# Four squares instead of three in a run of attention matmuls, from chunk 4 on, in a kernel of windowed attention and a feed-forward block

## The chip, the core and the metric

The kernel runs on one core of one Trainium2 chip. The metric is the device time of one execution in microseconds (us); the time of the kernel before is 961.14 us, the median of three runs. The profile is of one further execution.

## What is computed

Attention with 8 batches, 8 heads, 576 positions and head size 64 looks back over a window of 64 positions. Its output, 4608 rows of 512 numbers, goes through a feed-forward block with 2048 hidden units. All is in 32-bit floats.

```python
scores = scale * np.matmul(q, k.transpose(0, 1, 3, 2))
mask = (rel >= 0) & (rel < window)
attn = np.exp(scores - max); attn = attn / (np.sum(attn, axis=-1, keepdims=True) + 1e-09)
x = np.matmul(attn, v)  # 4608 x 512
h = x @ w_in            # 512 x 2048
out = (h * np.tanh(np.log1p(np.exp(h)))) @ w_out   # 2048 x 512
```

## The kernel before

**Chunks and steps.** The 4608 rows are cut into 12 chunks of 384 (CH). The feed-forward block takes a chunk in 16 steps (NF). One step is `ffn_in` (L208), 12 matmuls of 128x384 into one bank `h_ps` (three per quarter of the input, since inputs and weights are split into a high and a low part, `xh`, `xl` and `wi_h`, `wi_l`), and `ffn_out` (L246), nine matmuls of 128x512 into three accumulators `acc`. `ffn_out` runs two steps behind `ffn_in` (LAG). Between the two, the hidden values of a step pass through a chain: DVE takes `t` out of `h_ps` (L223), ACT applies four functions (L224, L229, L230, L231), DVE multiplies by `h_ps` again (L233), POOL splits the product into `gh` and `gl` (L237, L238). There are two banks of `h_ps`, so the chain of step n must have passed L233 before `ffn_in` of step n+2 can write that bank.

**Attention.** A chunk has 4 head pairs (NPAIR), and a pair has 3 squares: 128 queries (two blocks of 64) by 128 keys, for two heads. `att_scores` (L130) issues 12 matmuls for a pair into two banks `s_ps`; each is 64x64 by 128, in one corner of the array. Then come, for each of the 6 squares and heads, a masked minimum on DVE (L150, into `pr` and `mx`) and an exponential with its row sum on ACT (L153, into `pr` and `sm`), and for all six together the normalisation on DVE (L161 to L163). From chunk 3 on `att_transpose` (L166) transposes 32x32 pieces on DVE (L173, `pr` to `tr`) and puts the pieces in place with 12 small DMAs on SP's queue (L178, `tr` to `pT`). `att_values` (L190) issues 12 matmuls of 128x64 by 64 into a bank `o_ps`, the first of which waits for all 12 DMAs, and then ACT and DVE split the result into `xh` and `xl` (L205, L206).

A float32 matmul stands as two records in the trace, so the 12 matmuls of a pair appear as x24.

**What sets the order.** PE's order is the order of the program: the loop over steps at L405 calls `ffn_in` of step n, then the attention events that are due (`run(2 * n)`, L412), then `ffn_out` of step n-2, then `run(2 * n + 1)`. Half a step is a slot. `Att.plan` (L324) gives each pair of a chunk three events: scores at its slot, transpose 0.6 of a spacing later, values one spacing later, just ahead of the scores of the next pair. The attention of chunk c begins 6 slots ahead of the feed-forward block of chunk c-1 and must end 6 slots ahead of that of chunk c; from chunk 4 on that is 32 slots for 4 pairs (L401). Values of one pair and scores of the next so stand together, behind an `ffn_in`; I call this place a visit. The other engines' orders are laid out by a scheduler behind these events; the code of the feed-forward chain and of L205 and L206 has higher priority.

**Loads and buffers.** After the scores of pair p come the loads of `q_t` and `k_t` of pair p+2, after its values that of `v_t` (L297), each with two buffers. `pr` and `tr` share a ring of two (`tag="pr"`). There are two `pT`, zeroed once (L86). The output tiles `o` of `ffn_store` (L254) have a ring of three (`tag="st"`), used before that by the loading of weights. Attention has three PSUM banks (`tag="at"`).

Of the kernel before, what the change touches and what calls it, by code (L numbers as in the profile page):

```python
# [10 lines left out]
F32 = mybir.dt.float32  # L11
F32R = mybir.dt.float32r
# [3 lines left out]
ALU = mybir.AluOpType  # L16

P = 128
BLK = 64
TINY = float(np.array(0x38000000, np.uint32).view(np.float32))  # L20
BIG = float(np.array(0x47EFFFFF, np.uint32).view(np.float32))
SYNC = mybir.DependencyInfo(mybir.DependencyClass.Sync, mybir.DependencyReason.DATA)
SOON = 400
# [4 lines left out]
def tile_window_attn_mish_ffn(  # L28
# [10 lines left out]
    nc = tc.nc  # L39
    NPAIR, _, NT = qT.shape  # L40
    NF, _, NC_, _ = w_in.shape
    DO = w_out.shape[2]
    CH = 384
# [3 lines left out]
    NM = NB // 2  # L47
    HM = 2 * NM
    LAG = 2

    const = ctx.enter_context(tc.tile_pool(name="const", bufs=1))
    xp = ctx.enter_context(tc.tile_pool(name="xp", bufs=1))
    ap_ = ctx.enter_context(tc.tile_pool(name="ap_", bufs=2))
    mp = ctx.enter_context(tc.tile_pool(name="mp", bufs=2))
    ps_acc = ctx.enter_context(tc.tile_pool(name="ps_acc", bufs=1, space=bass.MemoryType.PSUM))
    ps_h = ctx.enter_context(tc.tile_pool(name="ps_h", bufs=2, space=bass.MemoryType.PSUM))
    ps_at = ctx.enter_context(tc.tile_pool(name="ps_at", bufs=3, space=bass.MemoryType.PSUM))
# [16 lines left out]
    for j in range(2):  # L74
        m = const.tile([P, P], F32, name=f"mask{j}")
# [7 lines left out]
    wo_l = const.tile([P, NF, DO], F32R, name="wo_l")  # L83


    pTs = [const.tile([P, P // 32, HM, 32], F32, name=f"pT{i}") for i in range(2)]  # L86
    for t in pTs:
        nc.gpsimd.memset(t, 0.0)
    pTs = itertools.cycle(pTs)


    order = []
    ordered = []

    def pe(*args, **kw):
        order.append(nc.tensor.matmul(*args, **kw).ins)  # L96

    def in_order():
        return tc.issue_after(order[-1]) if ordered else nullcontext()
# [6 lines left out]
    def bank(c, p, name):  # L106
        if c == 2 or (c == 0 and p % 2 == 0):
            return ps_acc.tile([P, CH], F32, name=name, tag=next(sums))
        return ps_at.tile([P, CH], F32, name=name, tag="at")
# [17 lines left out]
                                       ap=[[P, P], [BLK * P, NB], [1, P]]))  # L127
        return v_t

    def att_scores(c, p, tiles):  # L130
        q_t, k_t = tiles
        s_ps = [bank(c, p, "s_ps").rearrange("p (m k) -> p m k", k=P) for _ in range(2)]
        pr = ap_.tile([P, HM, P], F32, name="pr", bufs=2)
        mx = ap_.tile([P, HM], F32, name="mx", bufs=3)
        sm = ap_.tile([P, HM], F32, name="sm", bufs=3)
        for m in range(NM):
            for par, h in ((0, 0), (1, 1), (1, 0), (0, 1)):
                n = 2 * m + par
                rows = slice(h * BLK, (h + 1) * BLK)
                pe(s_ps[h][par * BLK:(par + 1) * BLK, m, :],  # L140
                   q_t[rows, n * BLK:(n + 1) * BLK], k_t[rows, n * BLK:n * BLK + P],
                                 start=True, stop=True)
        for h in range(2):
            js = slice(h * NM, (h + 1) * NM)
            for m in range(NM):
                first = [(c * NB + 2 * m + par) % blocks_per_seq == 0 for par in range(2)]
                mk = firsts[first.index(True)] if any(first) else mask
                j = h * NM + m

                nc.vector.tensor_tensor_reduce(  # L150
                    out=pr[:, j, :], in0=s_ps[h][:, m, :], in1=mk,
                    op0=ALU.add, op1=ALU.min, scale=-0.125, scalar=3.0e38, accum_out=mx[:, j:j + 1])
                nc.scalar.activation(pr[:, j, :], pr[:, j, :], AF.Exp, bias=mx[:, j:j + 1], scale=-1.0,  # L153
                                     accum_out=sm[:, j:j + 1])
            if c == 0:

                nc.vector.tensor_scalar(sm[:, js], sm[:, js], 1e-9, None, ALU.add)
                nc.vector.reciprocal(sm[:, js], sm[:, js])
                nc.vector.tensor_tensor(pr[:, js, :], pr[:, js, :], sm[:, js].unsqueeze(2).to_broadcast([P, NM, P]), ALU.mult)
        if c > 0:  # L160
            nc.vector.tensor_scalar(sm, sm, 1e-9, None, ALU.add)  # L161
            nc.vector.reciprocal(sm, sm)
            nc.vector.tensor_tensor(pr, pr, sm.unsqueeze(2).to_broadcast([P, HM, P]), ALU.mult)  # L163
        return pr

    def att_transpose(c, p, pr):  # L166
        pT = next(pTs)
        if c > 2:


            moved = []
            tr = ap_.tile([P, P // 32, HM, 32], F32, name="tr", tag="pr", bufs=2)
            nc.vector.transpose(tr.rearrange("p k j i -> p j k i"),  # L173
                                pr.rearrange("p j (k i) -> p j k i", i=32))
            for r in range(0, P, 32):
                for k in range(0, P, 32):
                    if 0 <= k - r % BLK <= BLK:
                        moved.append(nc.sync.dma_start(pT[k:k + 32, r // 32, :, :], tr[r:r + 32, k // 32, :, :]))  # L178
            return pT, moved
        for h in range(2):  # L180
            t_ps = (bank(c, p, "t_ps") if c else ps_h.tile([P, CH], F32, name="t_ps", tag="h_ps")
                    ).rearrange("p (m k) -> p m k", k=P)
            for m in range(NM):
                order.append(nc.tensor.transpose(t_ps[:, m, :], pr[:, h * NM + m, :], ident).ins)
            (nc.scalar.copy if h == 0 else nc.vector.tensor_copy)(
                pT[:, :, h * NM:(h + 1) * NM, :].rearrange("p r m i -> p m r i"),
                t_ps.rearrange("p m (r i) -> p m r i", i=32))
        return pT, []
# [101 lines left out]
    class Att:  # L290
# [17 lines left out]
        def scores(self, p):  # L308
            with in_order(), self.early():
                self.pr[p] = att_scores(self.c, p, self.qk[p])  # L310
            self.load(p + 2, "qk")

        def transpose(self, p):
            with in_order(), self.early():
                self.pT[p] = att_transpose(self.c, p, self.pr.pop(p))

        def values(self, p):
# [3 lines left out]
                att_values(self.c, p, self.v[p], self.pT.pop(p), self.x)  # L321
            self.load(p + 2, "v")

        def plan(self, begin, step, turn=0.6, lag=1):  # L324

            for p in range(NPAIR):
                at = begin + p * step
                events.extend([(at, 2, self.scores, p), (at + turn * step, 1, self.transpose, p),
                               (at + lag * step, 0, self.values, p)])

    events = []

    def run(slot):
        while events and events[0][0] <= slot:
            _, _, fn, p = events.pop(0)
            fn(p)
# [34 lines left out]
    starts = {c: 2 * len(steps) + 2 * NF * (c - 2) for c in range(2, NCHUNK)}  # L371
    steps += [(c, f) for c in range(2, NCHUNK) for f in range(NF)]

    atts = [Att(c) for c in range(NCHUNK)]
# [19 lines left out]
    ahead = 6  # L394
    begin = starts[2] + ahead - 1
    for c in range(3, NCHUNK):
        if c == 3:

            atts[c].plan(begin, (starts[c] - ahead - begin) / (NPAIR + 0.5), lag=1.5)
        else:  # L400
            atts[c].plan(begin, (starts[c] - ahead - begin) / NPAIR)  # L401
        begin = starts[c] - ahead
    events.sort(key=lambda e: e[:2])
    ordered.append(True)
# [52 lines left out]
```

## Time and profile before

| | |
|---|---|
| timed runs | 960.49, 961.14, 962.45 us |
| profiled execution, first to last instruction | 963.3 us |
| TensorE (PE) busy | 919.2 us, 95% |
| VectorE (DVE) busy | 491.9 us, 51% |
| ScalarE (ACT) busy | 622.1 us, 65% |
| GpSimd (POOL) busy | 330.3 us, 34% |
| granted PE clock, mean | 0.983 |

The span is the profiled execution's own time; no other time of it is known, and it stands 2.2 us above the median of the timed runs. In rows of the timeline the columns are the start in us from the span's start, the duration in us, the engine, the line and operation, what is written and read, the shape and the count (several instructions merged), and in brackets the idle time of the engine ahead of it with what ended it. PEld is the weight load on PE. SPq is the issuing of DMAs on SP's queue.

### The profile page before, as it was taken

Reading aid. Unit: us, or ns where it says so; the run is one execution under the profiler, and the core shown is the slowest. Engines: PE = TensorE matmul, PEld = TensorE weight load, DVE = VectorE, ACT = ScalarE, POOL = GpSimd, SP = SyncE. Lnnn points to the kernel's source line nnn. Section 1 sums busy time; section 2 is a strip of 40 time slices with the busy share of each in tenths; the row PEclk is TensorE's granted clock in tenths of the full one; section 3 lists DMA queues with packets and bytes.
Section 4 is the critical chain, followed back from the end, with each engine's and each line's share of the span. In section 5 each row is a group of like instructions: output and inputs, shape, how many; then the busy total and the mean of one; then the engine's idle time right before and its main releaser. Section 6 shows DMA issues by size and latency. Waiting matters only on the chain.

```text
span 963.3 us, 18036 instructions
## 1 busy us (share of the span) xinstructions
PE 919.2 (95%) x6408; PEld 812.7 (84%) x6408; DVE 491.9 (51%) x1352; ACT 622.1 (65%) x1525; POOL 330.3 (34%) x419
## 2 busy tenths in 40 slices
PE   4687899999999999999999999999999999999997
PEld 2576788978889988988898988898889888898996
DVE  6797788264545445444545444544544454442322
ACT  5575777676666666657666666665766756665664
POOL 2143555332333333333233233333333323333333
PEclk9789999999999999999999999999999999999999
DMA  7554332032233213213222222311312312300000
GB/s 246 158 195 137 131 104 73 22 117 84 78 89 101 56 51 107 61 54 90 76 55 79 85 56 67 97 53 54 115 51 55 114 50 56 96 16 13 33 1 34
DMA packets 82650, 77.35 MB, mean 80 GB/s; under 512 B 10368, under 2 KB 73856, under 8 KB 82560
## 3 DMA queue, kind: packets, MB, share of 16 engines
q1 hardware_dynamic: 82560, 76.19, 26.1%
q8 instruction: 51, 0.84, 0.4%
q14 instruction: 39, 0.32, 0.1%
HBM read 56.10 MB, written 9.44 MB: 68 GB/s over the span
## 4 chain that ended last, share of the span: by engine, by line
PE 79%; DVE 10%; ACT 4%; DMA 2%; issue 2%; SPq 2%; ACTq 0%; POOL 0%; DVEq 0%; POOLq 0%
PE h_ps L96 37%; PE acc L96 36%; PE o_ps L96 3%; PE s_ps L96 3%; DVE wa L277 2%; DMA st<-w_out 2%; SPq L178 1%; DVE wa L278 1%; DVE t L233 1%; ACT pr L153 1%; DVE wa L276 1%; DVE pr L150 1%; DVE pr L163 1%; ACT t L229 1%; DVE wa L274 1%
## 5 line engine op out<-in xcount | busy, mean ns | idle before, releaser
L96 PE MATMUL h_ps<-xh,wi_h 128*128 128x384 f32 x768 | 262.9, 342 | 5.6 <-DVE t L233 5.1
L224 ACT ACTIVATE t<-t 128x384 f32<-128x384 f32 x192 | 100.6, 524 | 259.3 <-DVE t L223 259.2
L237 POOL TENSOR_SCALAR gh<-t 128x384 fp32r<-128x384 f32 x176 | 90.8, 516 | 513.8 <-DVE t L233 491.5
L96 PE MATMUL h_ps<-xh,wi_l 128*128 128x384 f32 x768 | 259.8, 338 | 0.0
L96 PE MATMUL h_ps<-xl,wi_h 128*128 128x384 f32 x768 | 259.5, 338 | 0.0
L96 PE MATMUL acc<-wo_h,gh 128*128 128x512 f32 x576 | 230.3, 400 | 0.5 <-POOL gh L237 0.5
L96 PE MATMUL acc<-wo_l,gh 128*128 128x512 f32 x576 | 226.2, 393 | 0.0
L233 DVE SCALAR_TENSOR_TENSOR t<-t,h_ps 128x384 f32<-128x384 f32 x176 | 97.2, 552 | 237.9 <-ACT t L231 233.3
L238 POOL TENSOR_TENSOR gl<-t,gh 128x384 fp32r<-128x384 f32 x192 | 201.5, 1050 | 35.7 <-ACT gh L235 21.0
L96 PE MATMUL acc<-wo_h,gl 128*128 128x512 f32 x576 | 203.4, 392 | 0.0
L96 PEld LDWEIGHTS h_ps<-xh,wi_h 128*128 128x128 f32 x768 | 145.7, 190 | 18.0 <-DVE t L233 10.1
L96 PEld LDWEIGHTS h_ps<-xl,wi_h 128*128 128x128 f32 x768 | 145.9, 190 | 6.5
L96 PEld LDWEIGHTS h_ps<-xh,wi_l 128*128 128x128 f32 x768 | 145.7, 190 | 0.0
L223 DVE TENSOR_SCALAR t<-h_ps 128x384 f32<-128x384 f32 x192 | 106.4, 554 | 67.1 <-PE h_ps L96 65.3
L96 PEld LDWEIGHTS acc<-wo_h,gh 128*128 128x128 f32 x576 | 108.5, 188 | 23.9 <-issue 6.2
L96 PEld LDWEIGHTS acc<-wo_h,gl 128*128 128x128 f32 x576 | 108.5, 188 | 22.9
L96 PEld LDWEIGHTS acc<-wo_l,gh 128*128 128x128 f32 x576 | 108.7, 189 | 16.4 <-issue 0.2
L230 ACT ACTIVATE t<-t,half_b 128x384 f32<-128x384 f32 x192 | 118.2, 616 | 5.6
L229 ACT ACTIVATE t<-t,one_b 128x384 f32<-128x384 f32 x192 | 118.4, 617 | 4.3
L153 ACT ACTIVATE pr<-pr,mx 128x128 f32<-128x128 f32 x288 | 111.5, 389 | 10.5 <-DVE mx L150 10.5
L231 ACT ACTIVATE t<-t 128x384 f32<-128x384 f32 x192 | 100.1, 521 | 4.6
L150 DVE CUSTOM_DVE_ANT_0 pr<-s_ps,mask 128x128 f32<-128x128 f32 x288 | 64.8, 285 | 9.6 <-PE s_ps L96 9.6
(49 smaller groups left out, 666.3 us busy)
## 6 DMA issues: line engine op xcount, KB each, us to landing
v_t<-vN SPq DMA_DIRECT2D x48, 384.0 KB, 3.5
k_t<-kT SPq DMA_DIRECT2D x47, 224.0 KB, 3.6
pT<-tr SPq DMA_DIRECT2D x432, 24.0 KB, 1.8
out<-o SPq DMA_DIRECT2D x36, 256.0 KB, 2.3
q_t<-qT SPq DMA_DIRECT2D x47, 192.0 KB, 3.5
st<-w_in SPq DMA_DIRECT2D x16, 512.0 KB, 4.4
st<-w_out SPq DMA_DIRECT2D x16, 512.0 KB, 3.4
q_t<-qT SPq DMA_DIRECT2D x3, 64.0 KB, 2.2
```

The source lines that it names most:

```text
L96: order.append(nc.tensor.matmul(*args, **kw).ins)
L150: nc.vector.tensor_tensor_reduce(out=pr[:, j, :], in0=s_ps[h][:, m, :], in1=mk, op0=ALU.add, op1=ALU.min, scale=-0.125, scalar=3.0e38, acc ...
L153: nc.scalar.activation(pr[:, j, :], pr[:, j, :], AF.Exp, bias=mx[:, j:j + 1], scale=-1.0, accum_out=sm[:, j:j + 1])
L223: nc.vector.tensor_scalar(t, h_ps, 20.0, None, ALU.min)
L224: nc.scalar.activation(t, t, AF.Exp)
L229: nc.scalar.activation(t, t, AF.Square, bias=one_b)
L230: nc.scalar.activation(t, t, AF.Ln, bias=half_b, scale=0.5)
L231: nc.scalar.activation(t, t, AF.Exp, scale=-1.0)
L233: nc.vector.scalar_tensor_tensor(t, t, -1.0, h, ALU.add, ALU.mult)
L237: nc.gpsimd.tensor_scalar(gh, t, 1.0, 0.0, ALU.mult, ALU.add)
L238: nc.gpsimd.tensor_tensor(gl, t, gh.bitcast(F32), ALU.subtract)
L277: nc.vector.scalar_tensor_tensor(a, hi, 0xC0000000, a, ALU.bitwise_and, ALU.bitwise_or)
```

## The change

From chunk 4 on the attention of a chunk is no longer cut into 4 pairs of 3 squares but into 3 runs of 4 squares (`RUNS = NPAIR * NM // SQ`). A run takes the squares `4i` to `4i+3` of the chunk, from the `q_t`, `k_t`, `v_t` of two neighbouring pairs. So:

- 16 matmuls of scores, 8 minima and exponentials, one normalisation and one transpose of 128x1024, 12 DMAs of 32x256, 16 matmuls of values, and one split of 128x512 in a run, where a pair has 12, 6, 128x768, 12 of 32x192, 12, and 128x384;
- `plan_runs` puts the runs of a chunk at slots 0, 10 and 22 of its 32, and the transposes 0.6 of the spacing behind;
- `pr` and `tr` of a run are taken from the ring of three of the output tiles (`tag="st"`);
- there is one `pT` of 128x1024 for the runs, in the memory of the two small ones, zeroed anew in chunk 4 on POOL;
- after scores of run i come the loads of `q_t`, `k_t` of pair i+2, after those of the last run two pairs; the same for `v_t`.

Chunks 0 to 3 do what they did; `att_scores` and `att_transpose` now call the shared helpers `products`, `probs` and `moves`. Line numbers shift: L223, L233, L150, L163, L173, L206 of before are L267, L277, L161, L153, L193 and, in runs, L213 of the changed kernel.

```diff
+    SQ = DO // P
+    pT_all = const.tile([P, 2 * HM * P], F32, name="pT")
+    def pT_of(i, squares):
+        n = squares * P
+        return pT_all[:, i * n:(i + 1) * n].rearrange("p (r j i) -> p r j i", r=P // 32, i=32)
...
+    def run_scores(c, i, qk):
+        s_ps = [ps_at.tile([P, DO], F32, name="s_ps", tag="at").rearrange("p (m k) -> p m k", k=P) for _ in range(2)]
+        ms = range(i * SQ, (i + 1) * SQ)
+        for j, m in enumerate(ms):
+            products(qk[m // NM], m % NM, [s[:, j, :] for s in s_ps])
+        return probs(c, s_ps, [m % NM for m in ms], mp.tile([P, 2 * SQ, P], F32, name="pr", tag="st", bufs=3))
+    def run_transpose(pr):
+        pT = pT_of(0, 2 * SQ)
+        tr = mp.tile([P, P // 32, 2 * SQ, 32], F32, name="tr", tag="st", bufs=3)
+        nc.vector.transpose(tr.rearrange("p k j i -> p j k i"), pr.rearrange("p j (k i) -> p j k i", i=32))
+        return pT, moves(pT, tr)
+    def run_values(i, vs, pT, x):
+        pT, moved = pT
+        o_ps = ps_at.tile([P, DO], F32, name="o_ps", tag="at")
+        for j in range(SQ):
+            m = i * SQ + j
+            for par in range(2):
+                n = 2 * (m % NM) + par
+                for h in range(2):
+                    rows = slice(h * BLK, (h + 1) * BLK)
+                    pe(o_ps[rows, (2 * j + par) * BLK:(2 * j + par + 1) * BLK], vs[m // NM][:, n, rows],
+                       pT[:, 2 * par:2 * par + 2, h * SQ + j, :], start=True, stop=True)
...
+        xh, xl = (t.rearrange("p c n -> p (c n)")[:, i * DO:(i + 1) * DO] for t in x)
+        with tc.high_priority(offset=SOON):
+            nc.scalar.copy(xh, o_ps)
+            nc.vector.tensor_tensor(xl, o_ps, xh.bitcast(F32), ALU.subtract)
...
+        def run_transpose(self, i):
+            if self.c == 4 and i == 0:
+                nc.gpsimd.memset(pT_of(0, 2 * SQ), 0.0)
+            self.pT[i] = run_transpose(self.pr.pop(i))
...
+        def plan_runs(self, begin, end):
+            at = [begin + 2 * round((end - begin) * i / RUNS / 2) for i in range(RUNS + 1)]
+            for i in range(RUNS):
+                events.extend([(at[i], 2, self.run_scores, i), (at[i] + 0.6 * (at[i + 1] - at[i]), 1, self.run_transpose, i),
+                               (at[i + 1], 0, self.run_values, i)])
...
-            atts[c].plan(begin, (starts[c] - ahead - begin) / NPAIR)
+            atts[c].plan_runs(begin, starts[c] - ahead)
```

How the two orders read on PE and DVE, at one visit in the middle of the span. First PE, before, from the last matmul of an `ffn_in` (`h_ps`) over the visit to the first matmuls of the `ffn_out` behind it:

```order
L96 MATMUL h_ps<-xh_5624,wi_l 128x384
L96 MATMUL o_ps<-pT_107,v_t 64x64 x12
L96 MATMUL s_ps<-k_t,q_t 64x128 x12
L96 MATMUL acc_6531<-wo_h,gh 128x512
L96 MATMUL acc_6531<-wo_l,gh 128x512
L96 MATMUL acc_6531<-wo_h,gl 128x512
```

The same place in the changed kernel:

```order
L101 MATMUL h_ps<-xh_5598,wi_l 128x384
L101 MATMUL o_ps<-pT,v_t 64x64 x16
L101 MATMUL s_ps<-k_t,q_t 64x128 x16
L101 MATMUL acc_6450<-wo_h,gh 128x512
L101 MATMUL acc_6450<-wo_l,gh 128x512
L101 MATMUL acc_6450<-wo_h,gl 128x512
```

The visit has 16 and 16 matmuls in place of 12 and 12. From the first scores of chunk 4 to the last values of chunk 11 there are 24 spacings in place of 32: five, six and five steps lie between visits, where it was always four.

Then DVE behind the exponentials of a visit, before. `t_4292` and `t_4325` are the hidden values of the two steps that follow the visit:

```order
L161 TENSOR_SCALAR sm_4238<-sm_4238 128x6
L162 RECIPROCAL sm_4238<-sm_4238 128x6
L163 TENSOR_TENSOR pr_4236<-pr_4236,sm_4238 128x768
L223 TENSOR_SCALAR t_4292<-h_ps_4279 128x384
L173 STREAM_TRANSPOSE tr_4345<-pr_4236 128x6x4x32
L233 SCALAR_TENSOR_TENSOR t_4292<-t_4292,h_ps_4279 128x384
L223 TENSOR_SCALAR t_4325<-h_ps_4312 128x384
L233 SCALAR_TENSOR_TENSOR t_4325<-t_4325,h_ps_4312 128x384
```

And in the changed kernel, with `t_4401` and `t_4434` as those two steps:

```order
L151 TENSOR_SCALAR sm_4351<-sm_4351 128x8
L152 RECIPROCAL sm_4351<-sm_4351 128x8
L153 TENSOR_TENSOR pr_4349<-pr_4349,sm_4351 128x1024
L267 TENSOR_SCALAR t_4401<-h_ps_4388 128x384
L193 STREAM_TRANSPOSE tr_4478<-pr_4349 128x8x4x32
L267 TENSOR_SCALAR t_4434<-h_ps_4421 128x384
L277 SCALAR_TENSOR_TENSOR t_4401<-t_4401,h_ps_4388 128x384
L277 SCALAR_TENSOR_TENSOR t_4434<-t_4434,h_ps_4421 128x384
```

The multiplication and the transpose are a third wider, and the first operation on the second step's hidden values (L267 of `t_4434`) now stands ahead of the last one on the first step's (L277 of `t_4401`), where it stood behind it.

More of the change, by code (lines that the diff above doesn't have):

```diff
@@ L83, in tile_window_attn_mish_ffn @@
     wo_l = const.tile([P, NF, DO], F32R, name="wo_l")
[L86 to L89, printed above, removed]
+    SQ = DO // P
+    pT_all = const.tile([P, 2 * HM * P], F32, name="pT")
+    nc.gpsimd.memset(pT_all, 0.0)
+    def pT_of(i, squares):
+        n = squares * P
+        return pT_all[:, i * n:(i + 1) * n].rearrange("p (r j i) -> p r j i", r=P // 32, i=32)
+    pTs = itertools.cycle(pT_of(i, HM) for i in range(2))
     order = []
@@ L128, in load_v, with products, probs, normal @@
         return v_t
-    def att_scores(c, p, tiles):
+    def products(tiles, m, to):
         q_t, k_t = tiles
[L132 to L142, printed above, removed]
+        for par, h in ((0, 0), (1, 1), (1, 0), (0, 1)):
+            n = 2 * m + par
+            rows = slice(h * BLK, (h + 1) * BLK)
+            pe(to[h][par * BLK:(par + 1) * BLK, :],
+               q_t[rows, n * BLK:(n + 1) * BLK], k_t[rows, n * BLK:n * BLK + P], start=True, stop=True)
+    def probs(c, s_ps, ms, pr, halves=False):
+        ns = len(ms)
+        mx = ap_.tile([P, 2 * SQ], F32, name="mx", bufs=3)
+        sm = ap_.tile([P, 2 * SQ], F32, name="sm", bufs=3)
+        def normal(js):
+            w = js.stop - js.start
+            nc.vector.tensor_scalar(sm[:, js], sm[:, js], 1e-9, None, ALU.add)
+            nc.vector.reciprocal(sm[:, js], sm[:, js])
+            nc.vector.tensor_tensor(pr[:, js, :], pr[:, js, :], sm[:, js].unsqueeze(2).to_broadcast([P, w, P]), ALU.mult)
         for h in range(2):
-            js = slice(h * NM, (h + 1) * NM)
-            for m in range(NM):
+            for i, m in enumerate(ms):
                 first = [(c * NB + 2 * m + par) % blocks_per_seq == 0 for par in range(2)]
                 mk = firsts[first.index(True)] if any(first) else mask
-                j = h * NM + m
+                j = h * ns + i
                 nc.vector.tensor_tensor_reduce(
-                    out=pr[:, j, :], in0=s_ps[h][:, m, :], in1=mk,
+                    out=pr[:, j, :], in0=s_ps[h][:, i, :], in1=mk,
                     op0=ALU.add, op1=ALU.min, scale=-0.125, scalar=3.0e38, accum_out=mx[:, j:j + 1])
@@ L154, in att_scores @@
                                      accum_out=sm[:, j:j + 1])
[L155 to L163, printed above, removed]
@@ L164, in att_scores @@
-        return pr
+            if halves:
+                normal(slice(h * ns, (h + 1) * ns))
+        if not halves:
+            normal(slice(0, 2 * ns))
+        return pr
+    def att_scores(c, p, tiles):
+        s_ps = [bank(c, p, "s_ps").rearrange("p (m k) -> p m k", k=P) for _ in range(2)]
+        for m in range(NM):
+            products(tiles, m, [s[:, m, :] for s in s_ps])
+        return probs(c, s_ps, range(NM), ap_.tile([P, HM, P], F32, name="pr", bufs=2), c == 0)
+    def run_scores(c, i, qk):
[4 more added lines that the diff above has]
+        return probs(c, s_ps, [m % NM for m in ms], mp.tile([P, 2 * SQ, P], F32, name="pr", tag="st", bufs=3))
@@ new lines, in moves @@
+    def moves(pT, tr):
+        return [nc.sync.dma_start(pT[k:k + 32, r // 32, :, :], tr[r:r + 32, k // 32, :, :])
+                for r in range(0, P, 32) for k in range(0, P, 32) if 0 <= k - r % BLK <= BLK]
+    def run_transpose(pr):
[11 more added lines that the diff above has]
+                for h in range(2):
+                    rows = slice(h * BLK, (h + 1) * BLK)
+                    pe(o_ps[rows, (2 * j + par) * BLK:(2 * j + par + 1) * BLK], vs[m // NM][:, n, rows],
+                       pT[:, 2 * par:2 * par + 2, h * SQ + j, :], start=True, stop=True)
+                    for d in moved:
+                        tc.add_manual_dep(order[-1], d.ins.name, SYNC, reason="values in one piece")
+                    moved = []
+        xh, xl = (t.rearrange("p c n -> p (c n)")[:, i * DO:(i + 1) * DO] for t in x)
+        with tc.high_priority(offset=SOON):
+            nc.scalar.copy(xh, o_ps)
+            nc.vector.tensor_tensor(xl, o_ps, xh.bitcast(F32), ALU.subtract)
@@ L168, in att_transpose @@
         if c > 2:
-            moved = []
             tr = ap_.tile([P, P // 32, HM, 32], F32, name="tr", tag="pr", bufs=2)
@@ L174, in att_transpose @@
                                 pr.rearrange("p j (k i) -> p j k i", i=32))
[L175 to L179, printed above, removed]
+            return pT, moves(pT, tr)
         for h in range(2):
@@ L322, in values, with run_scores, run_values @@
             self.load(p + 2, "v")
+        def run_scores(self, i):
+            with in_order():
+                self.pr[i] = run_scores(self.c, i, self.qk)
+            self.load(i + 2, "qk")
+            if i == RUNS - 1:
+                self.load(NPAIR + 1, "qk")
+        def run_transpose(self, i):
+            if self.c == 4 and i == 0:
+                nc.gpsimd.memset(pT_of(0, 2 * SQ), 0.0)
+            self.pT[i] = run_transpose(self.pr.pop(i))
+        def run_values(self, i):
+            if self.x is None:
+                self.x = tuple(xp.tile([P, NC_, CH], F32R, name=f"x{n}{self.c % 2}") for n in "hl")
+            with in_order():
+                run_values(i, self.v, self.pT.pop(i), self.x)
+            self.load(i + 2, "v")
+            if i == RUNS - 1:
+                self.load(NPAIR + 1, "v")
+        def plan_runs(self, begin, end):
[3 more added lines that the diff above has]
+                               (at[i + 1], 0, self.run_values, i)])
         def plan(self, begin, step, turn=0.6, lag=1):
@@ L331, in tile_window_attn_mish_ffn @@
     events = []
+    RUNS = NPAIR * NM // SQ
     def run(slot):
```

## The prediction

> **What bounds the kernel now.** I read the page first: busy times, then the busy table by stretches for the stages, then the waits, then PE's timeline around the attention.
>
> ```profile
> span 963.3 us, 18036 instructions
> PE 919.2 (95%) x6408; PEld 812.7 (84%) x6408; DVE 491.9 (51%) x1352; ACT 622.1 (65%) x1525; POOL 330.3 (34%) x419
> 720.00:760.00 40.00, 40.00 (x281) 35.74 (x280) 18.47 (x53) 26.44 (x65) 13.54 (x18) 1.00 0.27 80
> PE h_ps L96 <- DVE t L233: 5.1, 3, 2.2
> ```
>
> In the stretch from 720 to 760 us, which stands for all from about 290 to 880 us, PE is busy for 40.00 of 40 us at a granted clock of 1.00, and DVE, ACT and POOL for 18, 26 and 14 us. The waits agree: in the whole span PE waits for the chain of hidden values (L233) three times, 5.1 us. So from chunk 4 on PE sets the pace, and a change there is worth what it takes from PE's own stream. In that stream a step without a visit is regular:
>
> ```profile
> 640.04 0.34 PE L96 MATMUL h_ps<-xh,wi_h 128*128 128x384 f32 x1
> 644.18 0.34 PE L96 MATMUL h_ps<-xh,wi_h 128*128 128x384 f32 x1
> 648.31 0.34 PE L96 MATMUL h_ps<-xh,wi_h 128*128 128x384 f32 x1
> ```
>
> These are the first matmuls of three `ffn_in`: (648.31 - 640.04) / 2 = 4.135 us a step. A visit looks like this, and the next row is the same place two visits later, undisturbed:
>
> ```profile
> 635.94 0.34 PE L96 MATMUL h_ps<-xh,wi_l 128*128 128x384 f32 x1
> 636.21 0.92 PE L96 MATMUL o_ps<-pT,v_t 128*64 128x64 f32 x24
> 637.06 0.89 PE L96 MATMUL s_ps<-k_t,q_t 64*64 64x128 f32 x24
> 637.87 0.50 PE L96 MATMUL acc<-wo_h,gh 128*128 128x512 f32 x1
> 638.21 0.39 PE L96 MATMUL acc<-wo_l,gh 128*128 128x512 f32 x1
> 638.44 0.40 PE L96 MATMUL acc<-wo_h,gl 128*128 128x512 f32 x1
> ...
> 673.41 0.92 PE L96 MATMUL o_ps<-pT,v_t 128*64 128x64 f32 x24
> 691.83 0.92 PE L96 MATMUL o_ps<-pT,v_t 128*64 128x64 f32 x24
> ```
>
> From visit to visit are 691.83 - 673.41 = 18.42 us; four steps are 16.54, so a visit costs PE 1.88 us.
>
> **What is in a visit.** The same rows cut off at later and later moments show how many records have come and when the last of them ends:
>
> ```profile
> 636.21 0.34 PE L96 MATMUL o_ps<-pT,v_t 128*64 128x64 f32 x4
> 636.21 0.80 PE L96 MATMUL o_ps<-pT,v_t 128*64 128x64 f32 x20
> 637.06 0.34 PE L96 MATMUL s_ps<-k_t,q_t 64*64 64x128 f32 x4
> 637.06 0.78 PE L96 MATMUL s_ps<-k_t,q_t 64*64 64x128 f32 x20
> ```
>
> Sixteen records of values, which are two squares, take 0.80 - 0.34 = 0.46 us, so 0.23 a square; scores 0.44, so 0.22 a square. Three squares are 3 x 0.45 = 1.35 us. The other 1.88 - 1.35 = 0.53 us belong to the visit, however many squares it has. The rows show where they are: the first values start 0.27 us behind the last `h_ps` matmul where the pitch is 0.17 (4.135 us less nine `acc` at 0.23, by twelve), the first two `acc` lie 0.34 apart where the pitch is 0.23, and the rest is where values end and scores begin and in the first matmuls of each kind.
>
> **The change, part by part.** *Fewer visits.* From the first scores of chunk 4 to the last values of chunk 11 the squares stay 96 (12 in each of 8 chunks), and the visits go from 32 to 24. Removed: 8 x 0.53 = 4.2 us. Bounds: were only the two edges towards `ffn_in` and `ffn_out` per visit and all else per square, it would be 8 x (0.10 + 0.11) = 1.7 us; the whole of a visit, 8 x 1.88 = 15, is excluded, since the squares stay. I take 4.2, since the cut-off rows show the cost of a square directly.
>
> The Trainium skill puts a number on such an end of a stream: by "TensorE: Matmul & The Clock Gate", section "Single matmul latency", a lone warm matmul takes (398 + N) / 2.4 ns, so about 166 ns beyond its columns. If each of the three changes of shape in a visit showed this once, that would be an estimate of 0.50 us a visit and 4.0 us in all; the trace's 0.53 decides.
>
> *The late DMAs.* Two visits of this execution begin late:
>
> ```profile
> 616.78 0.34 PE L96 MATMUL h_ps<-xh,wi_l 128*128 128x384 f32 x1
> 617.79 0.92 PE L96 MATMUL o_ps<-pT,v_t 128*64 128x64 f32 x24 [0.67 <-PE h_ps L96]
> 654.97 0.92 PE L96 MATMUL o_ps<-pT,v_t 128*64 128x64 f32 x24 [0.28 <-PE h_ps L96]
> 607.47 8.69 SPq L178 DMA_DIRECT2D pT<-tr  x12
> 644.81 8.65 SPq L178 DMA_DIRECT2D pT<-tr  x12
> 682.25 7.48 SPq L178 DMA_DIRECT2D pT<-tr  x12
> pT<-tr SPq DMA_DIRECT2D x432, 24.0 KB, 1.8
> ```
>
> The first begins 1.01 us behind the last `h_ps` matmul where 0.27 is the rule, the second at 654.97 where 636.21 + 18.42 = 654.63 was due: 0.74 and 0.34 us lost. The releaser named had long been done; both times the 12 DMAs took 8.7 us to issue in place of 7.48, and the last needs 1.8 us to land. In the ordinary case (644.81 + 7.48 + 1.8 = 654.1 at the latest, due 654.63) only half a microsecond is left. In the changed kernel the values come 23.0 us (five steps and a visit of 2.33 us) or 27.1 us behind their scores, not 18.42. The transpose ends later by about 1.3 us for the longer exponentials and multiplication (below) and 0.3 for its own length; the DMAs stay 12. So their slack grows to about 3 us, and even if a DMA of 32 KB took a third longer to issue (2.5 us in all), it covers that. I take out these stalls: 1.1 us in this execution. The timed runs may have had more or fewer, so I count half there: 0.6 (bounds 0 and 1.1).
>
> *The chain of hidden values.* This is where the longer run can hurt. PE's cover is that the chain of the step after the visit, which is queued on ACT behind the exponentials and on DVE behind the normalisation, must leave `h_ps` before `ffn_in` two steps later, here at 648.31:
>
> ```profile
> 639.74 0.39 ACT L153 ACTIVATE pr<-pr,mx 128x128 f32<-128x128 f32 x1
> 641.28 0.39 ACT L153 ACTIVATE pr<-pr,mx 128x128 f32<-128x128 f32 x1
> 641.57 0.19 ACT L153 ACTIVATION_READ_ACCUMULATOR pr<-pr,mx 128x1 f32 x1
> ...
> 641.79 0.42 DVE L161 TENSOR_SCALAR sm<-sm 128x6 f32<-128x6 f32 x1 [1.37 <-ACT pr L153]
> 642.47 0.96 DVE L163 TENSOR_TENSOR pr<-pr,sm 128x768 f32<-128x768 f32 x1
> 643.35 0.55 DVE L223 TENSOR_SCALAR t<-h_ps 128x384 f32<-128x384 f32 x1
> 643.82 0.97 DVE L173 STREAM_TRANSPOSE tr<-pr 128x768 f32<-128x768 f32 x1
> 646.35 0.55 DVE L233 SCALAR_TENSOR_TENSOR t<-t,h_ps 128x384 f32<-128x384 f32 x1 [1.56 <-ACT t L231]
> ```
>
> L233 ends at 646.90, 1.41 us before it is needed. In the changed kernel ACT has two more exponentials (four lie (641.28 - 639.74) apart, 0.385 each: 0.77), a split of 512 in place of 384 elements (0.12, from the 0.58 of L259 against 0.46 of L205 below) and the last function of the step ahead of all exponentials and not behind the first (about 0.1): 1.0 us. DVE's multiplication grows by a third of 0.96: 0.3. L223 of that step so begins 1.3 us later, and L233 after it; PE's own deadline moves by 0.45, the longer visit. Left: 1.41 - 1.3 + 0.45 = 0.55 us. The wider transpose (1.3 us) stands on DVE behind L223 and is done while ACT works on `t`. L267 of the second step, now ahead of L277 of the first, waits for its `h_ps`, which PE ends 10.6 us behind the visit's start (the visit and two pairs of `ffn_out` and `ffn_in`); it is through at about 11.4, just when ACT gives back the first step's `t`. Who is queued behind it: L277, `gh` and `gl` of the first step, which `ffn_out` needs 2.1 us after the deadline above. Cost taken: 0; the bounds are 0 and, for a chain 1 us longer than worked out, 0.45 us in each of 24 batches.
>
> *The ring.* The first minimum of a run (into `pr`) now waits, once a chunk, until an output tile has been stored.
>
> ```profile
> L259 ACT ACTIVATE o<-acc 128x512 f32<-128x512 f32 x24 | 13.7, 581 | 3.2 <-PE acc L96 3.2
> L205 ACT CAST xh<-o_ps 128x384 fp32r<-128x384 f32 x48 | 22.3, 464 | 8.5 <-PE o_ps L96 8.5
> out<-o SPq DMA_DIRECT2D x36, 256.0 KB, 2.3
> ```
>
> The accumulators are full one `ffn_in` (2.07 us) ahead of the visit, the copy takes 0.58, and the neighbour's store is issued first: by an estimate the store starts some 1 us ahead of the visit, and lands 2.3 us later. The minimum comes 3 us after the visit's start, behind values, scores and the split. Over 1 us is left; were it late, DVE would be held, with the chain behind it. Taken: 0, and its bound is inside that of the chain.
>
> *The rest.* Loads come a whole spacing ahead; a `v_t` is issued behind its values as before. The moves wait for the one `pT` to be read, which happens 10 us earlier. The zeroing in chunk 4 is one POOL instruction in an engine busy a third of the time, and bounded by a step's slack. Up to chunk 4 the order on every engine is that of before. All 0. The last chunk's feed-forward block runs alone and is the same.
>
> **The sum.** Against the profiled execution: 963.3 - 4.2 - 1.1 = 958.0 us of span. Against the median, which lies 2.2 us below that span: 961.14 - 4.2 - 0.6 = 956.3 us.
>
> **The rivals.** *Slower: `h_ps` comes free too late.* For it speaks that PE's slack in the chain shrinks from 1.41 to 0.55 us. It decides from the point at which ACT's batch and DVE's wide instructions together last 0.55 us longer than I worked out. At 1 us more PE would wait 0.45 us in each of 24 batches, 10.8 us, and the time would be 961.14 - 4.8 + 10.8 = 967 us. Against it stands a visit of before that has the output copies beside it:
>
> ```profile
> 609.43 0.54 DVE L233 SCALAR_TENSOR_TENSOR t<-t,h_ps 128x384 f32<-128x384 f32 x1
> 610.74 0.34 PE L96 MATMUL h_ps<-xh,wi_h 128*128 128x384 f32 x1
> ```
>
> There L233 ends at 609.97, 0.77 us ahead of the `ffn_in` that needs it, and PE does not wait. The Trainium skill states such a limit in "TensorEngine Tiling (Array Packing)", section "PSUM Bottleneck": packing small matmuls speeds up PE, not the emptying of PSUM, which may then bound. By that rule a larger run should move the wait to DVE and ACT; this trace has them busy 46% and 66% of the stretch from 720 to 760 us, so no row bears it out. Chance 0.07.
>
> *Most of the 0.53 us goes with the squares.* Then 1.7 us are saved and the stalls: 961.14 - 1.7 - 0.3 = 959.1, or 4.2 us are saved and short waits of 0.1 us a batch give 2.4 back: 958.7. The cut-off rows speak against the first. Chance 0.10.
>
> *The runs are not made as said.* The order on PE shows 16 and 16 matmuls, so this is out.
>
> **How the numbers follow.** My forecast has 0.80: 956.3 us; with stalls of 0 to 1.1, the spread of the runs before (0.7 below, 1.3 above the median) and a tenth of a microsecond here or there per visit (up to 1.5) it reaches from 954.5 to 958.5. With the second rival and a margin for the median of before the range is 954.4 to 959.6; what is left out is the slower case and the ends. A measurement of this kernel can tell about 0.2%, 1.9 us, from no change, so faster means below 959.2. Faster: the forecast and half the second rival, 0.85. The same: the other half, and 0.03 that I keep for what I don't see, 0.08. Slower: the first rival, 0.07.
>
> **What would show it.** In the profile after: visits of two rows x32, starting 23.0 and 27.1 us apart; x20 to x4 in the same 0.46 and 0.44 us; about 2.33 us a visit; no idle time in front of the values; L277 of the step behind a visit ending about half a microsecond ahead of its `ffn_in`. Waits of `h_ps` for L277 in every visit would make the first rival right; a visit of 2.5 us would mean that the fixed part was none.

## The result and the profile after

The changed kernel takes 956.32 us (median of five runs, 954.5 to 957.31), the kernel before, measured beside it, 961.14 us (five runs, 959.69 to 962.45). The ratio is 0.9947, with a 95% interval of 0.9932 to 0.9961: 4.8 us less, 0.5%, and so faster, as forecast. The forecast was 956.3 us.

The page of the changed kernel and its steady stretch, as a busy table (columns: PE, PEld, DVE, ACT, POOL, clock, DMA):

```profile
span 955.3 us, 17889 instructions
PE 916.9 (96%) x6408; PEld 812.6 (85%) x6408; DVE 479.3 (50%) x1312; ACT 624.5 (65%) x1517; POOL 330.7 (35%) x419
720.00:760.00 40.00, 40.00 (x310) 35.96 (x309) 20.15 (x61) 26.69 (x70) 12.81 (x18) 1.00 0.29 87
PE h_ps L101 <- DVE t L277: 3.4, 4, 2.2
```

PE still has no idle time in the steady stretch, it has the same 6408 matmul records, and in the whole span it waits 3.4 us for the chain of hidden values, not more than before. PE's timeline at three visits in a row:

```profile
648.33 0.34 PE L101 MATMUL h_ps<-xh,wi_l 128*128 128x384 f32 x1
648.60 1.15 PE L101 MATMUL o_ps<-pT,v_t 128*64 128x64 f32 x32
649.68 1.10 PE L101 MATMUL s_ps<-k_t,q_t 64*64 64x128 f32 x32
650.72 0.50 PE L101 MATMUL acc<-wo_h,gh 128*128 128x512 f32 x1
651.05 0.40 PE L101 MATMUL acc<-wo_l,gh 128*128 128x512 f32 x1
...
671.61 1.15 PE L101 MATMUL o_ps<-pT,v_t 128*64 128x64 f32 x32
698.76 1.15 PE L101 MATMUL o_ps<-pT,v_t 128*64 128x64 f32 x32
```

The visits lie 23.01 us (five steps) and 27.15 us (six steps) apart, with no idle time in front. With the step of 4.135 us a visit costs 23.01 - 20.68 = 2.33 us, where it was 1.88 with three squares: the fourth square adds 0.45 us, and 0.53 is left over as before. The same rows cut off early, as in the prediction:

```profile
648.60 0.34 PE L101 MATMUL o_ps<-pT,v_t 128*64 128x64 f32 x4
648.60 0.80 PE L101 MATMUL o_ps<-pT,v_t 128*64 128x64 f32 x20
649.68 0.34 PE L101 MATMUL s_ps<-k_t,q_t 64*64 64x128 f32 x4
649.68 0.78 PE L101 MATMUL s_ps<-k_t,q_t 64*64 64x128 f32 x20
```

Two squares take 0.46 and 0.44 us, to the digit as before. Where the two profiled executions differ is seen from the last values of chunk 3 (the visit with the first scores of chunk 4) and the last values of all. Before, then after:

```profile
285.60 0.92 PE L96 MATMUL o_ps<-pT,v_t 128*64 128x64 f32 x24 [0.80 <-DMA pT<-tr]
875.96 0.92 PE L96 MATMUL o_ps<-pT,v_t 128*64 128x64 f32 x24
```

```profile
282.98 0.92 PE L101 MATMUL o_ps<-pT,v_t 128*64 128x64 f32 x24 [1.23 <-DMA pT<-tr]
868.12 1.15 PE L101 MATMUL o_ps<-pT,v_t 128*64 128x64 f32 x32
```

From the one to the other are 590.36 us before and 585.14 after, 5.22 less. The two late visits of that execution of before are 1.08 of it, and the 4.14 left are the eight visits. The spans differ by 8.0 us; 2.6 of that lie ahead of chunk 4. There PE, DVE, ACT and the DMA queue run the same instructions in the same order in both kernels (POOL has one zeroing less at the start), and other profiles with that order differ as much (see the last section), so I do not count the 2.6 as an effect of the change. The profiled execution of after took 957.16 us with a span of 955.3, so some 1.9 us lie around the span. By the same addition the profiled execution of before took some 965.2 us, 4 us above its median: a span and a device time can't be set against each other as they stand, and that execution was not a typical one.

### The profile page after: what moved, and what is told of

Same layout as the page of the kernel before. It is cut to its first block, busy times and chain, and to the rows that moved or that the text cites. A ratio compares the mean times of both kernels' runs of the same rounds, so it can differ in the third digit from the quotient of the medians.

```text
span 955.3 us, 17889 instructions
## 1 busy us (share of the span) xinstructions
PE 916.9 (96%) x6408; PEld 812.6 (85%) x6408; DVE 479.3 (50%) x1312; ACT 624.5 (65%) x1517; POOL 330.7 (35%) x419
## 4 chain that ended last, share of the span: by engine, by line
PE 82%; DVE 10%; ACT 3%; issue 2%; DMA 2%; SPq 1%; ACTq 0%; POOL 0%; DVEq 0%; POOLq 0%
PE h_ps L101 37%; PE acc L101 37%; PE o_ps L101 4%; PE s_ps L101 3%; DVE wa L321 2%; DVE pr L153 1%; DVE wa L322 1%; DVE t L277 1%; DVE wa L320 1%; DVE pr L161 1%; DMA st<-w_out 1%; ACT t L273 1%; ACT wa L317 1%; DVE wa L318 1%; DVE wi_l L324 1%
## 5 line engine op out<-in xcount | busy, mean ns | idle before, releaser
L277 DVE SCALAR_TENSOR_TENSOR t<-t,h_ps 128x384 f32<-128x384 f32 x176 | 96.9, 551 | 219.0 <-ACT t L275 218.8
L101 PE MATMUL acc<-wo_h,gl 128*128 128x512 f32 x576 | 200.7, 392 | 0.0
L267 DVE TENSOR_SCALAR t<-h_ps 128x384 f32<-128x384 f32 x192 | 106.6, 555 | 87.1 <-PE h_ps L101 86.3
L161 DVE CUSTOM_DVE_ANT_0 pr<-s_ps,mask 128x128 f32<-128x128 f32 x288 | 65.5, 285 | 9.8 <-PE s_ps L101 9.7
```

Of the source, the lines that this page charges most:

```text
L161: nc.vector.tensor_tensor_reduce(out=pr[:, j, :], in0=s_ps[h][:, i, :], in1=mk, op0=ALU.add, op1=ALU.min, scale=-0.125, scalar=3.0e38, acc ...
L267: nc.vector.tensor_scalar(t, h_ps, 20.0, None, ALU.min)
L277: nc.vector.scalar_tensor_tensor(t, t, -1.0, h, ALU.add, ALU.mult)
```

## Experiments

All ratios are to the kernel before, with 95% intervals, and are to be held against the 0.9947 of the changed kernel.

**Three squares a run again (e1_three).** Everything of the change is kept but the size.

```diff
-    SQ = DO // P
+    SQ = 3
...
-        o_ps = ps_at.tile([P, DO], F32, name="o_ps", tag="at")
+        o_ps = ps_at.tile([P, SQ * P], F32, name="o_ps", tag="at")
...
-            if i == RUNS - 1:
+            if i == RUNS - 1 and RUNS < NPAIR:
```

> The changed kernel with three squares a run again: four runs a chunk, its ring, its single pT and its loads kept. Theory (a visit has a fixed cost of 0.53 us whatever its squares): 32 visits again, 18.42 us apart, so 8 x 0.53 = 4.2 us more than the changed kernel, and the values again only half a microsecond behind the last of the 12 DMAs, so now and then a visit begins late; about 960.5 us, ratio to the kernel before 0.998 to 1.001. Rival (the gain comes from the ring, the single pT or the placement of the loads): within 1 us of the changed kernel, 956 to 957 us, ratio 0.995.

Measured: 968.81 us, ratio 1.0083 (1.0068 to 1.0097), some 8 us above what the theory gave and 12 above the rival. The visits are 18.41 us apart again, three times out of four; the fourth time, once a chunk, they are 18.9 to 19.8 apart, 7 us more in all. The waits name the place, and ACT's timeline the cause:

```profile
PEld acc L101 <- ACT o L303: 8.0, 8, 1.5
PE acc L101 <- ACT o L303: 4.7, 8, 1.1
```

```profile
678.44 0.58 ACT L303 ACTIVATE o<-acc 128x512 f32<-128x512 f32 x1
681.38 0.60 ACT L303 ACTIVATE o<-acc 128x512 f32<-128x512 f32 x1 [1.20 <-DMA out<-o]
```

The third output copy of a chunk waits until the first output tile has been stored, and PE's next accumulation waits for that copy. With three squares a visit stands where the outputs are copied, so one of the three buffers of the shared ring holds a `pr` that is not yet transposed, and three output tiles must do with two. It is so in all eight chunks: the third copy begins 0.1 to 0.4 us after the first store issued has landed.

**Three squares with a ring of their own (e7_three_ring).** The edit of e1_three, and:

```diff
-    ... mp.tile([P, 2 * SQ, P], F32, name="pr", tag="st", bufs=3)
+    ... ap_.tile([P, 2 * SQ, P], F32, name="pr", tag="pr", bufs=2)
-        tr = mp.tile([P, P // 32, 2 * SQ, 32], F32, name="tr", tag="st", bufs=3)
+        tr = ap_.tile([P, P // 32, 2 * SQ, 32], F32, name="tr", tag="pr", bufs=2)
```

> Three squares a run as before in this series, single pT and loads of the changed kernel, but pr and tr in a ring of two of their own as in the kernel before. Theory (a visit has a fixed cost of 0.53 us, and the 7 us that the run with three squares and the shared ring took beyond the kernel before were waits for output tiles, which stand between pr and tr in that ring once a chunk): 32 visits 18.42 us apart, no wait of the accumulators for an output copy, about 961 us, ratio to the kernel before 0.998 to 1.002. Rival (the single pT or the loads cost the 7 us): ratio 1.007 or so, spacing over 18.42 at other places.

Measured: 961.09 us, ratio 1.0004 (0.9991 to 1.0016), as the theory had it. The visits are 18.42 us apart, and the wait of the accumulators is gone:

```profile
741.74 0.92 PE L101 MATMUL o_ps<-pT,v_t 128*64 128x64 f32 x24
760.16 0.92 PE L101 MATMUL o_ps<-pT,v_t 128*64 128x64 f32 x24
```

So the single `pT`, the loads and the new code together cost or gain nothing beyond the 1.5 us that the interval leaves. Between this kernel and the changed one lie the size of the runs and the ring that goes with it; no run has four squares with a ring of their own, but in the profile of the changed kernel no engine waits for an output tile.

**All runs two slots earlier (e8_ahead8).**

```diff
-    ahead = 6
-    begin = starts[2] + ahead - 1
+    ahead = 8
+    begin = starts[2] + 5
```

> The changed kernel with all runs from chunk 4 on two slots earlier, so that a visit, and with it a pr that is not yet transposed, stands where the output tiles are stored; chunk 3 gets 19 slots in place of 21. Theory (the shared ring costs nothing in the changed kernel only because of the place of its visits): the accumulators wait for an output copy once a chunk, 0.4 to 1.1 us each as in the run with three squares and that ring, 3 to 9 us in all, and chunk 3 loses 1 to 4 us for its late DMAs: 961 to 969 us, ratio to the kernel before 1.000 to 1.008. Rival (the ring does not matter with four squares): only chunk 3's loss, 957 to 960 us, and no waits from chunk 4 on.

Measured: 967.46 us, ratio 1.006 (1.0037 to 1.0083), inside what was expected. Rows of the waits show both parts, the ring and chunk 3; the last row is the stretch from 283 to 285 us, and below it stands the same stretch of the changed kernel (columns as in the busy table above):

```profile
PEld acc L101 <- ACT o L303: 7.0, 8, 2.3
PE o_ps L101 <- DMA pT<-tr: 4.6, 3, 3.0
...
283.00:285.00 2.00, 2.00 (x33) 1.67 (x30) 0.77 (x2) 0.34 (x1) 1.92 (x3) 0.50 0.39 118
```

```profile
283.00:285.00 2.00, 2.00 (x57) 1.76 (x58) 0.56 (x2) 1.03 (x3) 0.98 (x2) 1.00 0.00 0
```

From the visit beside the output copies to the next one are 27.45 to 30.91 us where six steps take 27.15 in the changed kernel, 7.5 us in all. Half of that is one chunk, where the first store took 3.9 us to land. Chunk 3 costs more than its wait: behind the 3.0 us without work the granted clock is 0.50 for a while, where it stays 1.00 behind the 1.23 us of the changed kernel, and the next visit comes another 1.5 us late. So the shared ring does no harm in the changed kernel because its visits stand 6 slots ahead of, 4 behind and 16 behind the start of a chunk's feed-forward block, and not beside the output copies, 2 behind it.

**Values and scores apart (e2_apart).**

```diff
-                               (at[i + 1], 0, self.run_values, i)])
+                               (at[i + 1] - 1, 0, self.run_values, i)])
```

> Four squares a run, but the values are issued one slot earlier, behind an ffn_out, and the scores stay behind the next ffn_in, so a visit is cut in two. Theory (the fixed part is paid where PE changes the shape of its matmuls: three changes in a joint visit, four in two separate ones; single visits of the early chunks in the profile of before show 0.36 us each beyond their squares, a joint one 0.53): 23 x 0.19 = 4.4 us more than the changed kernel, about 960.7 us, ratio to the kernel before 0.998 to 1.001. Rival (the fixed part is only the two edges towards ffn_in and ffn_out, 0.21 us each time): about the same, 23 x 0.21 = 4.8 minus what the change between values and scores costs. Second rival (the fixed part belongs to the run and not to the place): 0, ratio 0.995.

Measured: 961.80 us, ratio 1.0001 (0.9988 to 1.0015). PE's timeline shows the two halves, and the next values:

```profile
649.68 1.15 PE L101 MATMUL o_ps<-pT,v_t 128*64 128x64 f32 x32
650.77 0.44 PE L101 MATMUL h_ps<-xh,wi_h 128*128 128x384 f32 x1
...
653.05 1.10 PE L101 MATMUL s_ps<-k_t,q_t 64*64 64x128 f32 x32
...
672.88 1.15 PE L101 MATMUL o_ps<-pT,v_t 128*64 128x64 f32 x32
```

672.88 - 649.68 = 23.20 us, 0.19 more than in the changed kernel and as expected. Over 23 visits that is 4.4 us; the medians, of different sets of runs, lie 5.5 apart. The second rival, a fixed part that goes with the run wherever its halves stand, is out: three changes between kinds of matmuls cost 0.53 us, four cost 0.72. The first rival gives nearly the same number and is not told apart by this run. The rows of the changed kernel's visit do that. From the first values to the first scores are 1.08 us, of which four squares are 0.92; from there to the first `acc` are 1.04, of which they are 0.88. So 0.16 and 0.16 lie within the visit, beside 0.10 at each edge (0.27 less the pitch of 0.17, 0.33 less 0.23), and the four make up the 0.53 but for rounding.

**A longer chain behind the exponentials (e3_dve1, e4_dve3, e6_dve5).** One, three and five multiplications by 1.0 on half of `pr` stand ahead of the normalising one, and L267 of the next step is held behind that. The edit with one; with three the list is cut at `[:3 * (w == 8)]`, with five it has two more slices:

```diff
+            for half in (slice(4, 8), slice(0, 4), slice(4, 8))[:1 * (w == 8)]:
+                nc.vector.tensor_scalar(pr[:, half, :], pr[:, half, :], 1.0, None, ALU.mult)
...
+            if w == 8:
+                last.append(d)
...
+            while last:
+                tc.add_manual_dep(d.ins, last.pop().ins.name, SYNC, reason="behind")
```

> The changed kernel with one more multiplication by 1.0 of 128x512 on DVE in each of the 24 batches, ahead of the normalising multiplication, and the first operation on the next step's hidden values held behind it. It adds about 0.4 us to the chain of the step behind a visit. In the profile of the changed kernel that chain leaves h_ps 0.63 us ahead of the ffn_in that needs it. Theory (PE has that slack and no less): 0 to 0.5 us more than the changed kernel, ratio to the kernel before 0.994 to 0.996, and no waits of PE for the chain from chunk 4 on. Rival (the chain already bounds PE): 24 x 0.4 = 10 us more, ratio 1.005.

> The same with three such multiplications, about 1.2 us in the chain. Theory: the slack of 0.63 us is used up and PE waits about 0.5 to 0.6 us in each of the 24 batches: 12 to 15 us more than the changed kernel, 968 to 972 us, ratio to the kernel before 1.008 to 1.011. Rival (PE's slack is larger than the row shows, as the next steps absorb it): under 3 us more.

> The changed kernel with five further multiplications by 1.0 on DVE ahead of the normalising one. With three of them the chain of the step behind a visit came 0.57 us later (the rest was hidden in DVE's wait for the exponentials) and PE waited 0.12 us a visit, so the slack is about 0.45 us. Two more add 0.45 us each. Theory (beyond the slack every 0.1 us of the chain costs 0.1 us): the chain comes 1.47 us later, PE waits 1.0 us in each of 24 batches, 24 us more than the changed kernel, 978 to 983 us, ratio to the kernel before 1.017 to 1.023. Rival (PE makes part of it good): under 12 us more.

Measured: 957.12 us, ratio 0.9952 (0.9939 to 0.9965); 959.40 us, 0.9983 (0.9968 to 0.9997); 978.41 us, 1.018 (1.0159 to 1.020). The first is as the theory had it, without a wait of PE for the chain from chunk 4 on. The second missed by about 10 us: of the 1.2 us some 0.7 came into the chain, the rest was hidden in DVE's wait for the exponentials. It lands near the rival's 3 us, but not for the rival's reason, since the slack turns out smaller than the row shows. The third is inside its range. The changed kernel's chain, at the visit of 648.60 and at that of 671.61, then that with five:

```profile
656.98 0.55 DVE L267 TENSOR_SCALAR t<-h_ps 128x384 f32<-128x384 f32 x1
659.98 0.56 DVE L277 SCALAR_TENSOR_TENSOR t<-t,h_ps 128x384 f32<-128x384 f32 x1
661.17 0.34 PE L101 MATMUL h_ps<-xh,wi_h 128*128 128x384 f32 x1
...
682.88 0.54 DVE L277 SCALAR_TENSOR_TENSOR t<-t,h_ps 128x384 f32<-128x384 f32 x1
684.18 0.34 PE L101 MATMUL h_ps<-xh,wi_h 128*128 128x384 f32 x1
```

```profile
638.21 1.15 PE L102 MATMUL o_ps<-pT,v_t 128*64 128x64 f32 x32
650.99 0.55 DVE L284 SCALAR_TENSOR_TENSOR t<-t,h_ps 128x384 f32<-128x384 f32 x1 [1.12 <-ACT t L282]
651.60 0.44 PE L102 MATMUL h_ps<-xh,wi_h 128*128 128x384 f32 x1 [0.65 <-DVE t L284]
651.88 0.33 PE L102 MATMUL h_ps<-xl,wi_h 128*128 128x384 f32 x1
662.15 1.15 PE L102 MATMUL o_ps<-pT,v_t 128*64 128x64 f32 x32
```

The visit of 648.60, from which the expectations took their 0.63 us, is an exception: L277 begins 11.38 us behind its start there, and 682.88 - 671.61 = 11.27 (11.26 to 11.30) at the other 22 visits. Against these, with five it begins at 12.78, 1.51 later, and the visits are 23.94 apart, 0.93 more. With three it is 0.69 later and 0.12 more. Both give the same slack, 0.57 to 0.58 us, and beyond it the time goes one for one (0.82 more in the chain, 0.81 more between the visits). The row alone shows 684.18 - 683.42 = 0.76. Where the rest goes is seen with five: PE's matmul begins 0.06 us after L284 ends, and the next one comes 0.28 behind it where 0.17 is the pitch, so a wait costs PE some 0.17 beyond its idle time in the row.

**More DMAs ahead of the moves (e5_moves8).**

```diff
+        for n in range(8):
+            k, m = 32 * (n % 4), (8 + 2 * (n // 4)) * P
+            nc.sync.dma_start(pT_all[k:k + 32, m:m + 2 * P].rearrange("p (j i) -> p j i", i=32), tr[0:32, 0, :, :])
```

> The changed kernel with eight more DMAs of 32x256 on SP's queue ahead of the 12 of each run, into memory that nothing reads. At 0.59 us each they put the moves off by 4.7 us. In the profile of the changed kernel the moves are issued by 666.2 and land by 668.0 at the latest, and the values come at 671.61, 3.6 us later (runs five steps apart; 4.1 us more in runs six steps apart). Theory (slack of the moves is 3.6 to 4.2 us): the values of the 16 runs five steps apart begin 0.5 to 1.1 us late, those of the 8 runs six steps apart do not; 8 to 18 us more than the changed kernel, 964 to 974 us, ratio 1.003 to 1.013. Rival (values wait for something else than the moves): no change, ratio 0.995.

Measured: 976.38 us, ratio 1.0159 (1.0139 to 1.0179), somewhat over the expected span. The DMAs and the values behind them:

```profile
671.34 5.00 SPq L196 DMA_DIRECT2D pT<-tr  x8
676.38 7.56 SPq L187 DMA_DIRECT2D pT<-tr  x12
```

```profile
PE o_ps L101 <- DMA pT<-tr: 15.6, 14, 1.8
```

The eight take 5.0 us and not 4.7. The values of the runs five steps apart begin 0.7 to 1.9 us late, 1.15 on average and 18.5 us in all 16; those six steps apart hardly move (under 0.3). One of the 14 waits of the row is chunk 3's, as in the changed kernel. So values do wait for the moves, and the slack of the changed kernel is 5.0 - 1.15, some 3.8 us.

## Why the prediction was right, step by step

*Fewer visits, 4.2 us.* Right: 4.14 us in the two traces, 0.53 us a visit before and after, 0.45 a square. The run with three squares and its own ring is back at the time of before, with nothing else of the change undone but the ring. That the forecast and the median agree to 0.02 us is luck: the timed runs of the changed kernel alone spread over 2.8 us.

*The late DMAs, 0.6 us.* The mechanism is shown: no values of a run wait in the profile after, although a set of moves took its 8.7 us there too:

```profile
708.67 8.72 SPq L187 DMA_DIRECT2D pT<-tr  x12
721.77 1.15 PE L101 MATMUL o_ps<-pT,v_t 128*64 128x64 f32 x32
```

The values at 721.77 stand at their 23.01 us. The prediction's slack of about 3 us measures 3.8; its own terms (0.5 left, 4.6 more time, 1.6 later) add up to 3.5. How much the stalls were worth in the timed runs was only argued: the medians differ by 4.8, which fits 4.2 + 0.6, but runs spread by 2 to 3 us, and no run here separates the two. The half that the prediction took has no ground. The kernel with three squares and its own ring shows the stalls again at nearly the same place (0.7 us at one visit of its profile, near 612 us), and the last section shows that such places are not chance. If they come in every execution, the term is 1.1 and the sum 955.8 us, which is in the range as well.

*The chain of hidden values, 0.* Right, and its slack was close: 0.55 worked out, 0.76 in the row, 0.58 by experiment. The chain moved by 1.13 us (L233 began 10.14 us behind the visit's start, L277 begins 11.27) where 1.3 was worked out, and a slack read from rows leaves out the 0.17 above. The rival's mechanism is real: with 1.5 us more in the chain PE waits 0.93 us a visit, 22 us in all.

*The ring, 0.* The number held and the reason given was incomplete. The prediction looked at the first minimum of a run, which waits for a stored output tile. The wait that the ring can cause, and does with three squares or two slots earlier, is the other way round: an output copy waits for a buffer, and PE's accumulators for that copy. It costs 7 us where visit and copies meet. In the changed kernel they do not, so the term was 0; with other slots it would have been the largest.

*The sum against the span.* 958.0 was worked out and 955.3 seen. 2.6 us of the difference lie ahead of chunk 4, in a part that did not change. The prediction's 2.2 us between span and median set a span against a device time; that did not harm the forecast, which went from the median.

## What to carry to other kernels

In this kernel, where PE is busy all the time, the cost of a run of small matmuls that breaks into large ones has a part per run and a part per matmul; rows cut off at two moments separate them, and only the part per run is won by longer runs. Before making a batch longer, work out the slack of what is queued behind it on each engine, and let an experiment that adds a known delay confirm it, since only what reaches the chain counts. Read the row at several visits, since one of them can be an exception. A buffer ring shared by two uses is free only as long as their times do not meet; check that from where both stand in the program, in both directions.

## What was not expected of the hardware

Twelve small DMAs within the chip's memory take the same time to issue on SP's queue whether each moves 24 KB (7.48 us, in the prediction) or, in the changed kernel, 32 KB:

```profile
658.71 7.49 SPq L187 DMA_DIRECT2D pT<-tr  x12
```

Now and then a set takes 8.0 to 9.0 us, and this is not chance. The DMA view of before from 607 to 617 us, which holds the 8.69 us of the prediction, names a transfer of instructions on queue 8 beside the 12 DMAs (on queue 1; columns are packets, MB, share of the engines' time):

```profile
q1 hardware_dynamic: 570, 0.29, 12.5%
q8 instruction: 1, 0.02, 0.9%
```

From 658 to 666 us of the changed kernel, where the set takes 7.49, it names none. From 300 us on, in the nine profiles without extra DMAs, all 40 sets over 8.0 us hold such a transfer of 16 KB on queue 8, and no set without one takes over 7.92. The transfers come at nearly the same place from profile to profile: in the three with three squares all long sets but one begin between 583 and 684 us. That the transfer holds up the issuing is an inference; no run moves it.

And while PE's time from chunk 4 on repeats to 0.01 us a visit where nothing waits, the last values of chunk 3 begin between 280.5 and 285.6 us in the nine profiles whose order up to there is the same; the cause stays open.
